# Block-sorted attention and routed two-layer network on one core: values sorted as rows through DRAM for pairs 4-15, half-chunk blocks, three query turns during the Sinkhorn

## The chip, the core and the metric

The kernel runs on one core of a Trainium2 chip. The metric is device microseconds of one execution: three runs of the kernel before took 748.79, 749.36 and 750.04 us, so the median is 749.36 us. A separate execution was recorded by the hardware profiler. Its span, from the first to the last instruction, is 748.4 us, and that same run was timed at 750.19 us, so 1.8 us lie outside the span.

## What is computed

Attention comes first. For each of 32 heads (4 batches x 8 heads), queries, keys and values have 768 rows of 64. A small 8x8 matrix is normalised five times by rows and columns ("Sinkhorn"), and the result mixes the eight 96-row blocks of keys and of values. Each block of queries then attends to its own mixed block. The output, with the heads side by side, is a 3072x512 matrix x that goes through eight experts, weighted by a second normalised matrix.

```python
for _ in range(5):                      # P = sort_net, per head 8 x 8
    P = np.exp(P - P.max(-1))           # first round subtracts the maximum
    P = P / P.sum(-1); P = P / P.sum(-2)
k_sorted = einsum('bhij,bhjcd->bhicd', P, k_b)     # blocks of 96 rows
v_sorted = einsum('bhij,bhjcd->bhicd', P, v_b)
attn = softmax(scale * q_b @ k_sorted.T)           # per block
x = (attn @ v_sorted)  ->  3072 x 512
G = exp(x @ w_gate); 8 rounds of row and column normalisation
out = sum_e G[:, e] * (relu(x @ w1[e]) @ w2[e])    # 8 experts, 512 -> 1024 -> 512
```

## The kernel before

Two heads form a pair, and there are 16 pairs. The order of the instructions on every engine is written out by hand. Each engine runs its own instructions in that order, so an instruction that waits holds up everything behind it on its engine.

**Start.** DVE (VectorE) and ACT (ScalarE) alternate through the five Sinkhorn rounds (L123 to L136). Meanwhile PE (TensorE) runs 24 matmuls on zeros (L115, "spins") whose results nobody reads. The last product is written sixteen times wide (`Prep`, L135). Eight matmuls spread it over the partitions (L140), DVE copies it out (`Pbig`, L143), and `build_r` multiplies it with a mask into the mixing matrix `R` (L156).

**The pair loop** (L281) runs iterations m = 0 to 19 as a software pipeline. Iteration m holds `stage1(m)`, `stage2(m-1)`, `stage3(m-2)` and `stage4(m-3)`, with a `fill(1)` behind each stage.

- `stage1` (L162) sorts keys and values: 12 matmuls each with `R` as the moving operand (L171) leave them transposed (`KT`, `VT`, 64 columns per head). It also turns the queries by 12 transposes (L182), and builds `R` of the next pair.
- `stage2` (L189) makes the scores (16 matmuls, L197), the exponentials on ACT, and turns `VT` back into rows by 8 transposes (L204). DVE copies them to `VS`, which has a column of ones beside each head.
- `stage3` (L209) multiplies attention and values (16 matmuls, L216). DVE divides by the sum that the ones gave (L219, L220) into `OG`.
- `stage4` (L223) turns `OG` by 8 transposes (L227), and ACT writes it into `xtT`, the transposed x.
- `fill` (L268) puts in one block of the first expert layer (`h_block`: 4 matmuls of 512 columns and a relu on ACT or DVE) as soon as the batch that the block reads is done (`state["done"]`). Until the first batch is done, at m = 6, it puts in one spin instead.
- `gate` (L232) makes the gate's logits of one batch.

POOL (GpSimd) issues all loads of q, k, v and of the weights; they are cast from float32 to bfloat16 on the way. Four pairs are loaded ahead into five buffers (L79, L285). The first-layer weights of experts 0 and 1 are loaded at m = 0 and m = 5, the second-layer weights of these experts at m = 8 and m = 11. SP (SyncE) issues the load of `sort_net` and, at the end, the stores.

**After the loop** come eight normalisation rounds of the gate, with three blocks each (L313), and then the experts: `y_tile` (second layer, 8 matmuls of 512 columns, L339) alternates with the remaining `h_block`s; ten buffers `hT` limit how far the first layer runs ahead. The last tile's store ends the kernel.

Of the kernel before, what the change touches and what calls it, by code (L numbers as in the profile page):

```python
# [25 lines left out]
def kernel(  # L26
# [17 lines left out]
    HB = 10  # L44
    scale = 1.0 / (D ** 0.5)
# [6 lines left out]
    ps = ctx.enter_context(tc.tile_pool(name="ps", bufs=8, space=bass.MemoryType.PSUM))  # L52

    def bank(shape, dt=F32):
        return ps.tile(shape, dt, name="bank")
# [8 lines left out]

# [6 lines left out]
    mask = ones.tile([128, 16], F32)  # L71
    nc.vector.reduce_sum(out=mask, in_=ident.rearrange("p (j c) -> p c j", c=16), axis=AX.X)
# [6 lines left out]
    iop = actx.enter_context(tc.tile_pool(name="iop", bufs=5))  # L79
    atp_ = actx.enter_context(tc.tile_pool(name="atp", bufs=2))  # L80
    qkv = {}

    def load_pair(m):
        r = []
        for src, nm in ((kh, "kb"), (vh, "vb"), (qh, "qb")):
            t = iop.tile([128, 2, 6, 64], BF16, name=nm)
            nc.gpsimd.dma_start(out=t, in_=src[2 * m:2 * m + 2].rearrange("h p kk d -> p h kk d"))  # L87
            r.append(t)
        qkv[m] = r
# [11 lines left out]
    for m in range(4):  # L101
        load_pair(m)
# [3 lines left out]
    xtT = ones.tile([128, 4, B, 6, 128], BF16)  # L106
    xf = xtT.rearrange("d hp b kk p -> d hp (b kk p)")
# [4 lines left out]


    w_ = bank([128, 512])
    for _ in range(24):  # L115
        nc.tensor.matmul(w_, wide[:, 0:128], wide, start=True, stop=True)

    rs = ones.tile([32, 8], F32)
    Prep = ones.tile([32, 8, 8, 16], BF16)
    Pt = P.rearrange("p i j -> p j i")  # L120
    nc.vector.reduce_max(out=rs, in_=P, axis=AX.X)
    nc.vector.tensor_sub(P, P, mkap(rs, [rs.ap[0], rs.ap[1], [0, 8]]))
    for it in range(5):  # L123
        nc.scalar.activation(out=P, in_=P, func=AF.Exp)
        nc.vector.reduce_sum(out=rs, in_=P, axis=AX.X)
        nc.vector.reciprocal(out=rs, in_=rs)
        nc.vector.tensor_tensor(out=P, in0=P, in1=mkap(rs, [rs.ap[0], rs.ap[1], [0, 8]]),
                                op=ALU.mult)
        nc.vector.reduce_sum(out=rs, in_=Pt, axis=AX.X)
        nc.vector.reciprocal(out=rs, in_=rs)  # L130
        if it < 4:
            nc.vector.tensor_tensor(out=Pt, in0=Pt, in1=mkap(rs, [rs.ap[0], rs.ap[1], [0, 8]]),
                                    op=ALU.mult)
        else:
            nc.vector.tensor_tensor(out=Prep, in0=mkap(P, [P.ap[0], [8, 8], [1, 8], [0, 16]]),  # L135
                                    in1=mkap(rs, [rs.ap[0], [0, 8], [1, 8], [0, 16]]), op=ALU.mult)  # L136

    pbp = bank([128, 8, 32])
    for i in range(8):
        nc.tensor.matmul(pbp[:, i, :], Prep[:, i].rearrange("g j c -> g (j c)"),  # L140
                         ident[0:32, 0:32], start=True, stop=True)
    Pbig = ones.tile([128, 8, 32], F32)
    nc.vector.tensor_copy(Pbig, pbp)  # L143


    KT, VT, QT, ATT, VS, OG = {}, {}, {}, {}, {}, {}

    vs_ = [ones.tile([96, 8, 2, 65], BF16, name=f"vs{n}") for n in range(2)]
    for t in vs_:
        nc.vector.memset(t[:, :, :, 64:65], 1.0)  # L150

    Rt = {}

    def build_r(m):
        R = Rt[m] = atp_.tile([128, 2, 8, 16], BF16, name="R")
        nc.vector.tensor_tensor(  # L156
            out=R,
            in0=mkap(Pbig, [Pbig.ap[0], [1, 2], [32, 8], [0, 16]], off=2 * m),
            in1=mkap(mask, [mask.ap[0], [0, 2], [0, 8], [1, 16]]),
            op=ALU.mult)  # L160

    def stage1(m):  # L162
        kb, vb, qb = qkv[m]
        R = Rt[m]
        for src, dic, nm in ((kb, KT, "KT"), (vb, VT, "VT")):
            dic[m] = atp_.tile([128, 8, 6, 16], BF16, name=nm)
            for kh2 in range(2):
                b_ = bank([128, 3, 128])
                for k3 in range(3):
                    for h2 in range(2):  # L170
                        nc.tensor.matmul(b_[64 * h2:64 * h2 + 64, k3, :], src[:, h2, 3 * kh2 + k3, :],  # L171
                                         R[:, h2].rearrange("p i c -> p (i c)"), start=True, stop=True)
                dst = dic[m][:, :, 3 * kh2:3 * kh2 + 3, :].rearrange("d i kk c -> d kk i c")
                b_ = b_.rearrange("d kk (i c) -> d kk i c", c=16)
                if nm == "KT" or kh2 == 0:
                    nc.scalar.copy(dst, b_)  # L176
                else:
                    nc.vector.tensor_copy(dst, b_)  # L178
        b_ = bank([128, 6, 128], BF16)
        for kk in range(6):  # L180
            for h2 in range(2):
                nc.tensor.matmul(b_[64 * h2:64 * h2 + 64, kk, :], qb[:, h2, kk, :], ident,  # L182
                                 is_transpose=True, start=True, stop=True)
        QT[m] = atp_.tile([128, 6, 128], BF16, name="QT")
        nc.vector.tensor_copy(QT[m], b_)
        if m + 1 < NPAIR:
            build_r(m + 1)

    def stage2(m):  # L189
        ATT[m] = [atp_.tile([96, 2, 384], BF16, name=f"at{h2}") for h2 in range(2)]  # L190
        for half in range(2):
            bb = [bank([96, 4, 96]) for _ in range(2)]
            for i4 in range(4):
                i = half * 4 + i4
                for h2 in range(2):
                    hs = slice(64 * h2, 64 * h2 + 64)
                    nc.tensor.matmul(bb[h2][:, i4, :], KT[m][hs, i].rearrange("d kk c -> d (kk c)"),  # L197
                                     QT[m][hs, :, 16 * i:16 * i + 16], start=True, stop=True)
            for h2 in range(2):
                nc.scalar.activation(out=ATT[m][h2][:, half, :], in_=bb[h2].rearrange("k i q -> k (i q)"),  # L200
                                     func=AF.Exp, scale=scale)
        b_ = bank([96, 8, 128], BF16)
        for i in range(8):
            nc.tensor.matmul(b_[:, i, :], VT[m][:, i].rearrange("d kk c -> d (kk c)"), ident, is_transpose=True,  # L204
                             start=True, stop=True)
        VS[m] = vs_[m % 2]
        nc.vector.tensor_copy(VS[m][:, :, :, 0:64], b_.rearrange("c i (h d) -> c i h d", d=64))

    def stage3(m):  # L209
        OG[m] = atp_.tile([96, 8, 2, 64], BF16, name="OG")  # L210
        for half in range(2):
            for h2 in range(2):
                b_ = bank([96, 4, 65])
                for i4 in range(4):
                    i = half * 4 + i4
                    nc.tensor.matmul(b_[:, i4, :], ATT[m][h2][:, half, 96 * i4:96 * i4 + 96],  # L216
                                     VS[m][:, i, h2, :], start=True, stop=True)
                rc = atp_.tile([96, 4], F32, name="rc")
                nc.vector.reciprocal(out=rc, in_=b_[:, :, 64:65].rearrange("q i a -> q (i a)"))  # L219
                nc.vector.tensor_tensor(out=OG[m][:, 4 * half:4 * half + 4, h2, :], in0=b_[:, :, 0:64],  # L220
                                        in1=mkap(rc, [rc.ap[0], [1, 4], [0, 64]]), op=ALU.mult)

    def stage4(m):  # L223
        b, hpi = m // 4, m % 4
        b_ = bank([128, 8, 96], BF16)
# [3 lines left out]
        nc.scalar.copy(xtT[:, hpi, b].rearrange("d kk (i c) -> d i kk c", c=16),  # L229
                       b_.rearrange("d i (kk c) -> d i kk c", c=16))  # L230

    def gate(b):  # L232
        b_ = bank([128, 6, E])
        for t in range(6):
            for kk in range(4):
                nc.tensor.matmul(b_[:, t, :], xtT[:, kk, b, t, :], wg[:, kk], start=(kk == 0),  # L236
# [7 lines left out]
    def h_block(e, c, fb, both=False):  # L244
        if fb == 0:
            hT[e, c] = hp_.tile([128, 8, 512], BF16, name="hTs")
        b_ = bank([128, 512])
        for kk in range(4):
            nc.tensor.matmul(b_, w1t[e][:, kk, fb * 128:(fb + 1) * 128], xf[:, kk, c * 512:(c + 1) * 512],  # L249
                             start=(kk == 0), stop=(kk == 3))  # L250
        flip[0] ^= 1
        if both and flip[0]:
            nc.vector.tensor_scalar_max(hT[e, c][:, fb, :], b_, 0.0)  # L253
        else:
            nc.scalar.activation(out=hT[e, c][:, fb, :], in_=b_, func=AF.Relu)  # L255

    early = [(0, 0), (1, 0), (0, 1), (0, 2), (1, 1), (1, 2), (0, 3), (1, 3), (0, 4), (0, 5), (1, 4), (1, 5)]
    seq = early + [(e, c) for e in range(2, E) for c in range(6)]
    blocks = [(e, c, fb) for e, c in seq for fb in range(8)]
    last_batch = [0, 1, 1, 2, 3, 3]  # L260
    state = {"h": 0, "done": -1}

    def spin(n):
        b_ = bank([128, 512])
        for _ in range(n):
# [140 lines left out]
```

The softmax here doesn't subtract the row's maximum and nothing guards it: scores larger than these inputs give would overflow.

## Time and profile before

| | |
|---|---|
| median of three runs | 749.36 us |
| span of the profiled execution | 748.4 us (that run: 750.19 us) |
| PE matmul records | 4588, busy 738.3 us |
| 1536 + 1536 matmuls of the two expert layers | 346.1 + 338.0 us busy |
| first sorting matmul of the pair loop | starts at 14.45 us |
| start of iterations m = 0 to 7 | 14.45, 18.33, 22.46, 26.33, 30.62, 35.06, 39.27, 43.49 us |
| length of an iteration with four blocks and no gate | 6.81 us |
| first matmul of the second layer | 146.8 us |
| end of the last DVE instruction | 745.05 us |

Start times in a row of the timeline are microseconds from the span's start. A "busy" PE is not a PE at its peak: durations of matmuls overlap, so what one costs in a stream is read from the distance between the starts of consecutive groups. 32 matmuls of 512 columns take 6.91 us in the second half of the kernel, so one costs 0.216 us there.

### The profile page before, as it was taken

Reading aid. Unit: us, or ns where it says so; the run is one execution under the profiler, and the core shown is the slowest. Engines: PE = TensorE matmul, PEld = TensorE weight load, DVE = VectorE, ACT = ScalarE, POOL = GpSimd, SP = SyncE. Lnnn points to the kernel's source line nnn. Section 1 sums busy time; section 2 is a strip of 40 time slices with the busy share of each in tenths; the row PEclk is TensorE's granted clock in tenths of the full one; section 3 lists DMA queues with packets and bytes.
Section 4 is the critical chain, followed back from the end, with each engine's and each line's share of the span. In section 5 each row is a group of like instructions: output and inputs, shape, how many; then the busy total and the mean of one; then the engine's idle time right before and its main releaser. Section 6 shows DMA issues by size and latency. Waiting matters only on the chain.

```text
span 748.4 us, 10663 instructions
## 1 busy us (share of the span) xinstructions
PE 738.3 (99%) x4588; PEld 358.5 (48%) x4588; DVE 252.1 (34%) x497; ACT 274.2 (37%) x497; POOL 48.9 (7%) x71
## 2 busy tenths in 40 slices
PE   6999999999999999999999999999999999999997
PEld 3776665444444444444444444444444444444443
DVE  5887775632122122122221221221221221212443
ACT  2776665513423423324324324234234233243000
POOL 8542000000000000000000000000000000000000
PEclk8999999999999999999999999999999999999999
DMA  9999100011300061200330032100330003000133
GB/s 149 204 205 163 19 2 1 1 20 38 56 1 1 0 96 29 46 1 1 56 57 1 0 57 40 19 0 1 57 56 1 1 0 57 1 0 1 43 154 141
DMA packets 29679, 33.21 MB, mean 44 GB/s; under 512 B 1984, under 2 KB 22464, under 8 KB 29632
## 3 DMA queue, kind: packets, MB, share of 16 engines
q0 software_dynamic: 26128, 26.23, 22.5%
q1 hardware_dynamic: 3504, 6.30, 2.2%
q8 instruction: 36, 0.59, 0.3%
q14 instruction: 11, 0.09, 0.0%
HBM read 52.45 MB, written 6.29 MB: 78 GB/s over the span
## 4 chain that ended last, share of the span: by engine, by line
PE 98%; DMA 1%; POOL 1%; DVE 0%; issue 0%; POOLq 0%
PE bank L249 44%; PE bank L339 44%; PE bank L171 2%; PE bank L216 2%; PE bank L204 1%; PE bank L197 1%; PE bank L266 1%; DMA qb<-in_q_dram 1%; PE bank L182 1%; PE bank L227 1%; PE bank L236 0%; POOL kb L87 0%; POOL vb L87 0%; PE bank L321 0%; POOL qb L87 0%; DVE osbl L345 0%
## 5 line engine op out<-in xcount | busy, mean ns | idle before, releaser
L255 ACT ACTIVATE hTs<-bank 128x512 bf16<-128x512 f32 x358 | 213.7, 597 | 371.2 <-PE bank L249 370.4
L249 PE MATMUL bank<-xtT,w1e 128*128 128x512 bf16 x1536 | 346.1, 379 | 0.0
L339 PE MATMUL bank<-w2e,hTs 128*128 128x512 bf16 x1536 | 338.0, 379 | 0.0
L345 DVE SCALAR_TENSOR_TENSOR osbl<-bank,glog,osbl 128x512 f32<-128x512 f32 x168 | 126.2, 751 | 398.7 <-PE bank L339 398.7
L339 PEld LDWEIGHTS <-hTs 128*128 128x128 bf16 x1536 | 150.2, 98 | 181.0
L249 PEld LDWEIGHTS <-w1e 128*128 128x128 bf16 x1536 | 147.9, 98 | 170.3
L342 DVE TENSOR_SCALAR osbl<-bank,glog 128x512 f32<-128x512 f32 x24 | 18.0, 751 | 54.7 <-PE bank L339 54.7
L220 DVE TENSOR_TENSOR OG<-bank,rc 96x256 bf16<-96x256 f32 x64 | 26.9, 421 | 2.2
L95 POOL DMA_DIRECT2D w1e<-in_moe_w_dram x8 | 6.0, 752 | 312.6 <-PE bank L249 312.3
L99 POOL DMA_DIRECT2D w2e<-in_moe_w_dram x8 | 7.1, 888 | 237.5 <-PE bank L339 237.1
L253 DVE TENSOR_SCALAR hTs<-bank 128x512 bf16<-128x512 f32 x26 | 17.7, 683 | 6.1 <-PE bank L249 6.1
L229 ACT COPY xtT<-bank 128x768 bf16<-128x768 bf16 x16 | 12.8, 798 | 14.1 <-PE bank L227 13.7
L176 ACT CAST KT<-bank 128x384 bf16<-128x384 f32 x32 | 13.8, 486 | 8.1 <-PE bank L171 7.9
L87 POOL DMA_DIRECT2D kb<-in_k_dram x16 | 11.5, 722 | 20.9 <-PE bank L171 20.1
L178 DVE CAST VT<-bank 128x384 bf16<-128x384 f32 x16 | 8.9, 553 | 11.2 <-PE bank L171 8.8
L219 DVE RECIPROCAL rc<-bank 96x4 f32<-96x4 f32 x64 | 10.9, 171 | 3.7 <-PE bank L216 3.7
L87 POOL DMA_DIRECT2D vb<-in_v_dram x16 | 11.5, 722 | 5.2 <-PE bank L266 2.5
L87 POOL DMA_DIRECT2D qb<-in_q_dram x16 | 11.6, 724 | 1.9 <-issue 0.3
L266 PE MATMUL bank<-wide 128*128 128x512 bf16 x28 | 10.6, 419 | 0.0
L204 PE MATMUL bank<-ident,VT 128*96 128x128 bf16 x128 | 10.4, 224 | 0.0
L171 PE MATMUL bank<-R,kb 128*64 128x128 bf16 x192 | 9.1, 234 | 1.0 <-DMA qb<-in_q_dram 1.0
L197 PEld LDWEIGHTS <-KT 64*96 64x96 bf16 x256 | 7.1, 121 | 5.8 <-issue 5.6
(152 smaller groups left out, 232.6 us busy)
## 6 DMA issues: line engine op xcount, KB each, us to landing
w1e<-in_moe_w_dram POOLq DMA_DIRECT2D x8, 1024.0 KB, 8.1
w2e<-in_moe_w_dram POOLq DMA_DIRECT2D x8, 1024.0 KB, 8.9
out_dram<-osbl SPq DMA_DIRECT2D x24, 256.0 KB, 2.0
kb<-in_k_dram POOLq DMA_DIRECT2D x16, 192.0 KB, 7.3
vb<-in_v_dram POOLq DMA_DIRECT2D x16, 192.0 KB, 7.3
qb<-in_q_dram POOLq DMA_DIRECT2D x16, 192.0 KB, 7.3
P<-in_sort_net_dram SPq DMA_DIRECT2D x1, 8.0 KB, 1.7
wg<-in_moe_w_gate_dram POOLq DMA_DIRECT2D x1, 8.0 KB, 6.8
```

The source lines that it names most:

```text
L87: nc.gpsimd.dma_start(out=t, in_=src[2 * m:2 * m + 2].rearrange("h p kk d -> p h kk d"))
L171: nc.tensor.matmul(b_[64 * h2:64 * h2 + 64, k3, :], src[:, h2, 3 * kh2 + k3, :], R[:, h2].rearrange("p i c -> p (i c)"), start=True, stop= ...
L204: nc.tensor.matmul(b_[:, i, :], VT[m][:, i].rearrange("d kk c -> d (kk c)"), ident, is_transpose=True, start=True, stop=True)
L216: nc.tensor.matmul(b_[:, i4, :], ATT[m][h2][:, half, 96 * i4:96 * i4 + 96], VS[m][:, i, h2, :], start=True, stop=True)
L220: nc.vector.tensor_tensor(out=OG[m][:, 4 * half:4 * half + 4, h2, :], in0=b_[:, :, 0:64], in1=mkap(rc, [rc.ap[0], [1, 4], [0, 64]]), op=AL ...
L249: nc.tensor.matmul(b_, w1t[e][:, kk, fb * 128:(fb + 1) * 128], xf[:, kk, c * 512:(c + 1) * 512], start=(kk == 0), stop=(kk == 3))
L253: nc.vector.tensor_scalar_max(hT[e, c][:, fb, :], b_, 0.0)
L255: nc.scalar.activation(out=hT[e, c][:, fb, :], in_=b_, func=AF.Relu)
L266: nc.tensor.matmul(b_, wide[:, 0:128], wide, start=True, stop=True)
L339: nc.tensor.matmul(b_, hT[e, c][:, fb, tt * 128:(tt + 1) * 128], w2t[e][:, fb, :], start=(fb == 0), stop=(fb == 7))
L342: nc.vector.tensor_scalar(out=osbl[:, t, :], in0=b_, scalar1=glog[:, t, e:e + 1], scalar2=None, op0=ALU.mult)
L345: nc.vector.scalar_tensor_tensor(out=osbl[:, t, :], in0=b_, scalar=glog[:, t, e:e + 1], in1=osbl[:, t, :], op0=ALU.mult, op1=ALU.add)
```

## The change

- **Values of pairs 4 to 15** (`MB = 4`). A second mixing matrix `Rv`, with its columns in another order, is the stationary operand of two matmuls of 384 columns. The result has rows as partitions (`VR`), and is copied out half by ACT and half by DVE. It is written to a DRAM tile `vd` by SP and read back, in the order that `stage3` wants, into `VS` (`v_back`, also SP). The 8 transposes of `VT` and the copy to `VS` fall away for these pairs.
- **Start.** The 24 spins become 4, and 6 in each Sinkhorn round. The queries of pairs 0 to 2 (`QA = 3`) are turned in rounds 1 to 3, copied out by ACT between two exponentials. The loads start with these queries. The wide product `Prep` is replaced by a narrow one (`Pb`), one matmul that turns it, and eight matmuls with a selection matrix `sel` (a copy on ACT). `R` of pair 0 is built from PSUM before `Pbig` is copied.
- **Blocks.** Chunk 1 of experts 0 and 1 and chunk 4 of expert 0 are cut into halves of 256 columns.
- **Buffers and order.** One PSUM tile of eight banks is handed out in turn. `stage3` takes two banks at a time and divides per head, not per head and half. Five pairs are loaded ahead into six buffers. The weight loads move: first layer to m = 1 and m = 4, second layer to m = 13 and m = 15, later first-layer weights to where the last block of the expert two before was issued. The gate of a batch comes at the end of m = 8, 12, 16, 19. The last tile of the second layer is cut into halves. Code for a DRAM path of the output (`XB = 16`) is not reached.

```diff
+    PS = ps.tile([128, 8, 512], F32)
+    def bank(dt=F32):
+        b_ = PS[:, turn[0] % 8, :]
+        turn[0] += 1
...
-    for m in range(4):
-        load_pair(m)
+    for src, m in ((qh, 0), (qh, 1), (kh, 0), (vh, 0), (qh, 2), (kh, 1), (vh, 1), (kh, 2), (vh, 2),
+                   (qh, 3), (kh, 3), (vh, 3)) + tuple((s_, m) for m in range(4, AH) for s_ in (kh, vh, qh)):
+        load(src, m)
...
-    for _ in range(24):
-        nc.tensor.matmul(w_, wide[:, 0:128], wide, start=True, stop=True)
+    sel = ones.tile([64, 64, 16], BF16)
+    nc.scalar.copy(sel, mkap(ident, [[ident.ap[0][0], 64], [1, 64], [0, 16]]))
+    spin(4)
     for it in range(5):
         nc.scalar.activation(out=P, in_=P, func=AF.Exp)
+        if 1 <= it <= QA:
+            q_turn(it - 1, "act")
+        spin(SQ_)
         nc.vector.reduce_sum(out=rs, in_=P, axis=AX.X)
...
-            nc.vector.tensor_tensor(out=Prep, in0=mkap(P, [P.ap[0], [8, 8], [1, 8], [0, 16]]),
-                                    in1=mkap(rs, [rs.ap[0], [0, 8], [1, 8], [0, 16]]), op=ALU.mult)
+        dst = Pt if it < 4 else Pb.rearrange("p (i j) -> p j i", j=8)
+        nc.vector.tensor_tensor(out=dst, in0=Pt, in1=rbi, op=ALU.mult)
+    nc.tensor.matmul(b_, Pb, ident[0:32, 0:32], start=True, stop=True)
+    nc.vector.tensor_copy(PT, b_)
+    for i in range(8):
+        nc.tensor.matmul(pbp[:, i, :], sel[:, 8 * i:8 * i + 8, :].rearrange("k j c -> k (j c)"), PT,
+                         start=True, stop=True)
+    build_r(0, pbp[:, :, 0:2].rearrange("p i g -> p g i"))
+    nc.vector.tensor_copy(Pbig, pbp.rearrange("p i g -> p g i"))
...
     def stage1(m):
+        sort_t(KT, "KT", kh, m, "aa")
+        if m < MB:
+            sort_t(VT, "VT", vh, m, "ad")
+        else:
+            VR = atp_.tile([128, 6, 2, 64], BF16, name="VR")
+            t = qkv[id(vh), m]
+            for h2 in range(2):
+                b_ = bank()[:, 0:384]
+                nc.tensor.matmul(b_, Rv[m][:, h2].rearrange("p c i -> p (c i)"),
+                                 t[:, h2].rearrange("p kk d -> p (kk d)"), start=True, stop=True)
+                b_ = b_.rearrange("p (kk d) -> p kk d", d=64)
+                if h2 == 0:
+                    nc.scalar.copy(VR[:, :, h2, :], b_)
+                else:
+                    nc.vector.tensor_copy(VR[:, :, h2, :], b_)
+            vd[m] = drp.tile([6, 128, 128], BF16, name="vd")
+            nc.sync.dma_start(out=vd[m].rearrange("kk p e -> p kk e"), in_=VR.rearrange("p kk h d -> p kk (h d)"))
+        if m >= QA:
+            q_turn(m, "dve")
...
+    def v_back(m):
+        if m >= MB:
+            VS[m] = vs_[m % 3]
+            nc.sync.dma_start(out=VS[m][:, :, 1:129],
+                              in_=vd[m].rearrange("kk (c i) e -> (kk c) i e", i=8))
...
+    early = [(0, 0, 0, 512), (1, 0, 0, 512), (0, 1, 0, 256), (1, 1, 0, 256), (0, 1, 256, 512), (1, 1, 256, 512),
+             (0, 2, 0, 512), (1, 2, 0, 512), (0, 3, 0, 512), (1, 3, 0, 512), (0, 4, 0, 256), (0, 4, 256, 512),
+             (0, 5, 0, 512), (1, 4, 0, 512), (1, 5, 0, 512)]
...
     for m in range(NPAIR + 4):
         if m < NPAIR:
             stage1(m)
-        if m + 4 < NPAIR:
-            load_pair(m + 4)
-        if m == 0:
+        if m + AH < NPAIR:
+            load(kh, m + AH)
+            load(vh, m + AH)
+            load(qh, m + AH)
+        if m == 1:
             load_w1(0)
-        if m == 5:
+        if m == W1B:
             load_w1(1)
-        if m == 8:
+        if m == 13:
             load_w2(0)
-        if m == 11:
+        if m == 15:
             load_w2(1)
-        fill(1)
+        fill(f[0], spins=SP_)
         if 1 <= m <= NPAIR:
             stage2(m - 1)
+        if m < NPAIR:
+            v_back(m)
...
+        if m in (6, 10, 14, 19 if XB < NPAIR else 18):
+            state["done"] += 1
+        fill(f[3], spins=SP_)
+        if m in (8, 12, 16, 19):
+            gate({8: 0, 12: 1, 16: 2, 19: 3}[m])
```

## The prediction

> **What bounds the kernel.** I read the page's slices first, then the chain of waits, then PE's timeline of one iteration.
>
> ```profile
> PE   6999999999999999999999999999999999999997
> PEclk8999999999999999999999999999999999999999
> DMA  9999100011300061200330032100330003000133
> PE 98%; DMA 1%; POOL 1%; DVE 0%; issue 0%; POOLq 0%
> ```
>
> From 14.45 us to the end PE is the chain: 98% of the span. So the end moves by what PE's work between is worth, and by when it starts. Two other things show: in the first slice the clock is not full, and in the first four slices the DMA engines are full. PE's own timeline prices the work. Iteration m = 8, with four blocks (columns: start, length, what):
>
> ```profile
> 50.89 0.53 PE L171 MATMUL bank<-R,kb 128*64 128x128 bf16 x12
> 51.25 0.50 PE L171 MATMUL bank<-R,vb 128*64 128x128 bf16 x12
> 51.59 0.50 PE L182 MATMUL bank<-ident,qb 128*64 128x128 bf16 x12
> 52.02 1.04 PE L249 MATMUL bank<-xtT,w1e 128*128 128x512 bf16 x4
> 52.99 0.56 PE L197 MATMUL bank<-QT,KT 64*96 64x96 bf16 x16
> 53.48 0.65 PE L204 MATMUL bank<-ident,VT 128*96 128x128 bf16 x8
> 53.96 1.03 PE L249 MATMUL bank<-xtT,w1e 128*128 128x512 bf16 x4
> 54.82 0.33 PE L216 MATMUL bank<-vs_194,at_1144 96*96 96x65 bf16 x4
> ```
>
> Distances between starts: key sort 0.36, value sort 0.34, query turn 0.43, scores 0.49, value transposes 0.48, a block 0.86. A block takes 0.97 where a stage with another array shape follows: a switch of shape costs about 0.1. An iteration takes 6.81, without its blocks 3.35; four spins (0.216 each) instead make 4.21, as iterations 5 and 6 show. No fill with a finished batch ever runs dry: all 28 spins of L266 lie in m = 0 to 6.
>
> The start is worse than its work. Stretches of the start (columns after the span: busy time of PE, PEld, DVE, ACT, POOL; then granted clock, DMA share, GB/s):
>
> ```profile
> 6.80:13.70 6.90, 2.90 (x20) 1.34 (x19) 5.26 (x20) 0.54 (x3) 5.68 (x8) 1.00 1.24 179
> 13.70:20.50 6.80, 6.05 (x77) 4.31 (x76) 2.69 (x8) 2.49 (x6) 4.60 (x7) 0.50 1.39 200
> ```
>
> PE has nothing to do from 9.34 to 13.11 us. Then the granted clock is 0.50 for 6.8 us, just when the pairs begin: a spin takes 0.43 instead of 0.216, and iterations 0 and 1 take 3.88 and 4.13.
>
> **The sum, against the span of 748.4.**
>
> (a) First sorting matmul. Before, the last exponential starts at 10.33 and `R` is ready at 14.39. ACT's new copy `sel` (64x1024) costs about 1.0 by the rows of 384 and 768 elements (0.487, 0.798) and waits for the identity at 2.47, so the first exponential moves from 2.95 to 3.5. A round is 1.81, so the next two are due at 5.3 and 7.1. Each query turn puts a copy of 0.80 (L229's row) on ACT ahead of the next exponential, and it needs its load. The first five loads landed at 4.9, 7.6, 8.5, 9.5 and 10.55 (issue plus time to landing). The queries of pairs 0, 1 and 2 become loads 1, 2 and 5. Turn 1 (7.6 + 0.8 for PE at a slow clock + 0.8) puts the fourth exponential at 9.2, and turn 2 (10.55 + 0.45 + 0.8) the fifth at 11.8. Then 1.51 to the last product as before, 0.26 for it (L132's row; `Prep` cost 1.21), 0.3 for one matmul and its hand-over, 0.2 for a small copy, 0.45 for eight matmuls, 0.45 for `R`: 15.1. That is +0.65. Bounds: 13.6 if no load is waited for and `sel` hides, 17 if every turn runs at the slow clock.
>
> (b) Iterations 0 to 6 took 29.04. At the full clock, with the queries of three pairs gone: m = 0: 0.36 + 0.34 + 0.86 + a switch or so = 1.70; m = 1 adds stage 2: 2.75; m = 2 is 4.21 without query turn and stage 4: 3.44; m = 3 is 4.21. At m = 4 values are sorted as rows: 384 columns are 0.162 by the 512-column price, twice 0.324, plus two switches of 0.10 (keys and queries beside it use the 64-column shape) against 0.34: +0.18, so 4.39. m = 5 also loses the transposes (0.48): 3.91. m = 6 the same, and one spin becomes a block (+0.65): 4.56. Together 24.96: -4.1. The bounds of the switch are 0 and 0.2 per pair, since the trace has no such sequence; I take 0.2, what the two observed switches cost. ACT needs 3.65 per iteration here (4.21 minus 0.56 idle, iteration 6) and DVE 4.2, less 0.6 when the copy to `VS` goes, plus 0.4 for `Rv`; neither exceeds PE by more than 0.3, which the eight banks absorb.
>
> (c) The rows of pairs 7 to 15: 9 x 0.18 = +1.6. The transposes of pairs 6 to 15: 10 x 0.48 = -4.8.
>
> (d) The block moved into m = 6 is missing later: -0.86.
>
> (e) Half blocks: 96 more matmuls. Their columns are the same; 128 columns cost 0.060 at L204 against 0.054 by the 512-column price, so 6 ns each at most: +0.3 (0 to 0.6). As no fill ran dry, they bring nothing.
>
> (f) Last tile in halves: DVE's last 0.75 becomes about 0.42 (L220's row of 256 elements), and a smaller store: -0.4 (0 to -0.6).
>
> Sum: 0.65 - 4.1 + 1.6 - 4.8 - 0.86 + 0.3 - 0.4 = -7.6. From the median 749.36 (0.83 below the profiled run's 750.19, of which 1.8 lie outside the span) this gives **741.8**.
>
> Costed at nothing: the fewer, wider divisions of `stage3` and the moved gate (DVE and ACT wait for PE in the blocks: 398.7 us at L345, 370.4 at L255), three memsets on POOL (0.2 each, ahead of loads needed 10 us later), second-layer weights at m = 13 and 15 (needed at 140, landing after 12 at most).
>
> **What the trip through DRAM hides behind.** Per pair SP issues a write and a read (0.38 each by the issue of `sort_net`), and its queue is empty until the first store at 705 us. The read waits for the write; behind it on SP is only the next pair's write. `VS` of pair 4 is wanted 2.6 us into m = 6, some 9.7 after `VR` is copied. A landing on an idle queue took 1.7 to 2.0; with the engines shared, say 3.4, twice, plus two issues: 7.6. So it hides with 2 us to spare, later with 6 or more. The other bound is the 7.3 median of the loads, which counts a queue eight deep: then pair 4 is 5.7 late.
>
> It also takes DMA engines that are full. Each trip is 2 x 768 runs of 256 bytes. Two neighbouring microseconds of the DMA view price them:
>
> ```profile
> DMA packets 278, 0.20 MB, mean 201 GB/s; under 512 B 17, under 2 KB 278, under 8 KB 278
> DMA packets 649, 0.19 MB, mean 185 GB/s; under 512 B 416, under 2 KB 649, under 8 KB 649
> w1e<-in_moe_w_dram POOLq DMA_DIRECT2D x1, 1024.0 KB, 12.2
> ```
>
> In the first, 261 load packets (1536 bytes read each) fill 16 engines: 61 ns apiece. In the second, 28 fewer of them made room for 399 packets of 16 bytes: 4 ns apiece. A 256-byte packet lies between 4 and 61; by bytes, 61 x 256/1536 + 4 = 14.5 ns, my value, so 0.7 us a leg. The third row is expert 1's weights: issued at 34.06, landed at 46.3, behind saturated loads. In the changed kernel the same loads stand before it, plus eight legs of pairs 4 to 7: 46.3 + 5.6 = 51.9. PE wants it in the ninth block, the last fill of m = 8: 40.1 + 6.5 + 5.6 = 52.2. It just arrives; every ns per packet above 15.3 costs 0.38 us.
>
> [...]
>
> **Rivals.**
>
> *The start is lost again.* PE still idles while the last round ends (about 1.3 us from 12.3), and waits for turn 2. Busy time before the boundary at 13.7 is some 4.6 of 6.8 us: between the 2.90 that led to half clock and the 6.05 that led to full. If it counts as idle, 15.1 to 20.5 runs at half clock: 5.4/2 = +2.7. With the first sort 1.5 later as well: 746. Still faster.
>
> [...] The one fall in this trace followed a gap of 3.77.
>
> *The trip starves the loads.* If 256-byte packets cost nearly what 1536-byte packets do, the first-layer weights and then the pairs come late, and PE stalls in order. Gain and loss cancel at 15.3 + 7.6/0.38 = 35 ns. At 61 ns the weights land at 46.3 + 23.4 = 69.7, 17.5 late: 759; at 45 ns: 753. For it: DMA share above 1.2 until 60 us. Against it: the 4 ns, and that loads past m = 8 have 9 us of slack. This is the slower case.
>
> *Rows don't pay.* If the switches and an exposed weight load eat the whole 0.48 per pair, 3.6 less is gained: 745.4. That is inside the range.
>
> **How the numbers follow.** The forecast with its own bounds (738.5 to 745) gets 0.62, the lost start (745 to 747.5) 0.18, the starving loads (above 749.4 mostly, 753 to 759) 0.14, and 0.06 is left for partial stalls that end near the old time. A measurement can tell 0.2%, or 1.5 us, from no change. So faster 0.80, same 0.06, slower 0.14. The range leaves the starving case out above and reaches 738 below (no switch cost -2.4, first sort at 14): 738 to 748.
>
> **What would show it.** Right: the clock stays at 1.00 from 7 us on; first sorting matmul near 15.1, m = 7 near 40; iterations of 6.5; ACT's fifth exponential just after the third turn's copy. Wrong: PE waiting for `w1e`, `vs` or `kb` between 28 and 90 us; a row of 0.50 after 13 us; switches of more than 0.1 round the two new matmuls; DMA packets under 512 bytes whose mean time is nearer 61 than 15 ns.

## The result and the profile after

The changed kernel takes 766.88 us (median of 4 runs, 766.69 to 767.78) against 749.24 us for the kernel before on the same chip: 1.0237 times as long, interval 1.0219 to 1.0254. The forecast was 741.8, the range ended at 748. The span of the profiled execution is 765.0 us, 16.6 more than before.

The slices of PE and of the granted clock (40 equal parts of the span, each digit in tenths), and the shares of the chain, on the page of the changed kernel:

```profile
PE   7959799999999999999999999999999999999998
PEclk9979899999999999999999999999999999999999
PE 92%; DMA 5%; issue 1%; DVE 1%; POOL 1%; ACT 0%; POOLq 0%; DVEq 0%; SPq 0%; ACTq 0%
```

PE fell from 98% of the chain to 92%, and DMA has 5%. PE's slices 3 and 5 are low, and the clock is with them. The waits name what PE stood for (columns: total, times, longest):

```profile
PE PS L274 <- DMA vs_264<-vd: 8.3, 1, 8.3
PE PS L274 <- DMA vs_263<-vd: 5.2, 1, 5.2
```

L274 is `stage3`, and `vs<-vd` is the sorted values coming back from DRAM. The timeline of PE shows both stands, of pair 4 in iteration 6 and of pair 9 in iteration 11 (in brackets the idle time and what ended it):

```profile
42.15 0.38 PE L134 MATMUL PS<-wide 128*128 128x512 bf16 x1
50.82 0.85 PE L274 MATMUL PS<-vs_264,at_766 96*96 96x65 bf16 x8 [8.29 <-DMA vs_264<-vd]
...
92.37 0.85 PE L274 MATMUL PS<-vs_263,at_1374 96*96 96x65 bf16 x8 [5.16 <-DMA vs_263<-vd]
```

After each stand PE runs at half clock. The stretches of the two stands and of what follows (busy time of PE, PEld, DVE, ACT, POOL, then granted clock, DMA share, GB/s):

```profile
42.50:50.80 8.30, 0.02 (x1) 0.00 (x0) 0.80 (x3) 1.23 (x4) 2.25 (x4) 0.71 1.21 198
50.80:56.20 5.40, 5.38 (x43) 3.28 (x43) 2.38 (x5) 1.36 (x3) 0.03 (x1) 0.50 1.29 195
...
87.20:92.40 5.20, 0.04 (x2) 0.03 (x1) 0.04 (x1) 0.84 (x3) 0.00 (x0) 0.80 0.96 148
92.40:97.10 4.70, 4.70 (x38) 3.90 (x39) 2.02 (x5) 1.18 (x2) 0.00 (x0) 0.50 0.46 85
```

5.4 and 4.7 us at half clock lose 2.7 and 2.4 us. A shorter wait of 0.9 us follows at 59.3 us, for pair 5. The profile puts it down to DVE, but the read of these values, issued at 54.88, landed 5.3 us later, at 60.2, just when the matmul starts. Together the trip's waits and the half clock behind them cost some 19 us on this trace.

The difference between the two traces, piece by piece (first matmuls of the iterations, and the end of the last DVE instruction: 745.05 before, 761.95 after):

| stretch | before | after | difference | forecast |
|---|---|---|---|---|
| to the first sorting matmul | 14.45 | 17.37 | +2.9 | +0.65 |
| iterations 0 to 5 | 24.82 | 22.60 | -2.2 | -4.4 |
| iteration 6 | 4.22 | 15.04 | +10.8 | +0.34 |
| iterations 7 to 14 | 55.63 | 62.92 | +7.3 | -2.4 |
| from iteration 15 on | 645.93 | 644.02 | -1.9 | -1.8 |

The SP queue shows the legs of the trip. A write is issued, the read waits for its landing, and the next pair's write stands behind the read:

```profile
32.81 0.40 SPq L243 DMA_DIRECT2D vd<-VR  x1
41.59 0.66 SPq L289 DMA_DIRECT2D vs_264<-vd  x1
42.34 0.57 SPq L243 DMA_DIRECT2D vd<-VR  x1
54.88 0.56 SPq L289 DMA_DIRECT2D vs_265<-vd  x1
...
73.35 0.59 SPq L243 DMA_DIRECT2D vd<-VR  x1
84.77 0.55 SPq L289 DMA_DIRECT2D vs_263<-vd  x1
```

The write of pair 4 is issued at 32.81; its read can go only at 41.59, and lands at 50.8: 8.7 and 9.2 us for the two legs that the forecast took for 3.4 each. Pair 5's rows lay ready at about 37.7, but their write had to wait behind that read until 42.34. For pair 9 the write alone took 11.4 us. Beside it, from POOL's timeline:

```profile
73.21 1.80 POOL L115 DMA_DIRECT2D w2e<-in_moe_w_dram  x2
```

Both second-layer loads go out at 73.2 us, in iteration 9, though they stand at m = 13 and 15 in the program: POOL goes through its own list as fast as its own waits let it, and behind the last pair's loads nothing held it.

### The profile page after: what moved, and what is told of

The parts are those of the page before. It is cut to its first block, busy times and chain, and to the rows that moved or that the text cites. A ratio compares the mean times of both kernels' runs of the same rounds, so it can differ in the third digit from the quotient of the medians.

```text
span 765.0 us, 10470 instructions
## 1 busy us (share of the span) xinstructions
PE 737.4 (96%) x4412; PEld 362.7 (47%) x4486; DVE 242.9 (32%) x440; ACT 277.9 (36%) x515; POOL 49.1 (6%) x74
## 4 chain that ended last, share of the span: by engine, by line
PE 92%; DMA 5%; issue 1%; DVE 1%; POOL 1%; ACT 0%; POOLq 0%; DVEq 0%; SPq 0%; ACTq 0%
PE PS L327 43%; PE PS L430 43%; PE PS L274 1%; DMA vs_264<-vd 1%; DMA vd<-VR 1%; DMA vs_263<-vd 1%; DMA vb<-in_v_dram 1%; DMA qb<-in_q_dram 1%; PE PS L216 1%; PE PS L257 1%; PE PS L305 1%; PE PS L143 1%; PE PS L235 1%; PE PS L314 0%; DVE OG L278 0%
## 5 line engine op out<-in xcount | busy, mean ns | idle before, releaser
L333 ACT ACTIVATE hTs<-PS 128x512 bf16<-128x512 f32 (+1 forms) x372 | 215.2, 579 | 397.7 <-PE PS L327 382.5
L327 PE MATMUL PS<-xtT,w1e 128*128 128x512 bf16 (+1 forms) x1595 | 346.5, 369 | 2.0 <-issue 0.2
L430 PE MATMUL PS<-w2e,hTs 128*128 128x512 bf16 (+1 forms) x1513 | 336.0, 378 | 1.6
L436 DVE SCALAR_TENSOR_TENSOR osbl<-PS,glog,osbl 128x512 f32<-128x512 f32 (+1 forms) x169 | 126.4, 748 | 398.3 <-PE PS L430 375.6
L433 DVE TENSOR_SCALAR osbl<-PS,glog 128x512 f32<-128x512 f32 x24 | 18.0, 751 | 51.2 <-PE PS L430 50.2
L331 DVE TENSOR_SCALAR hTs<-PS 128x512 bf16<-128x512 f32 (+1 forms) x36 | 20.3, 570 | 23.2 <-PE PS L327 22.1
L278 DVE TENSOR_TENSOR OG<-PS,rc 96x512 bf16<-96x512 f32 x32 | 22.0, 687 | 1.1
L134 PE MATMUL PS<-wide 128*128 128x512 bf16 x55 | 19.0, 462 | 1.4 <-DVE wide L85 1.2
L221 ACT CAST KT<-PS 128x384 bf16<-128x384 f32 x32 | 13.8, 484 | 9.7 <-PE PS L216 9.0
L307 ACT COPY xtT<-PS 128x768 bf16<-128x768 bf16 x16 | 12.7, 796 | 11.5 <-PE PS L305 10.7
L104 POOL DMA_DIRECT2D kb<-in_k_dram x16 | 11.5, 722 | 21.1 <-PE PS L235 10.6
L104 POOL DMA_DIRECT2D vb<-in_v_dram x16 | 11.7, 728 | 10.6 <-DMA w1e<-in_moe_w_dram 4.5
```

Source lines behind the costliest of these rows:

```text
L134: nc.tensor.matmul(b_, wide[:, 0:128], wide, start=True, stop=True)
L278: nc.vector.tensor_tensor(out=OG[m][:, :, h2, :].rearrange("q (f i) d -> q f i d", f=2), in0=b_[:, :, :, 1 - h2:65 - h2], in1=mkap(rc, [rc ...
L331: nc.vector.tensor_scalar_max(hT[e, c][:, fb, lo:hi], b_, 0.0)
L333: nc.scalar.activation(out=hT[e, c][:, fb, lo:hi], in_=b_, func=AF.Relu)
L430: nc.tensor.matmul(b_, hT[e, c][:, fb, tt * 128:(tt + 1) * 128], w2t[e][:, fb, ns], start=(fb == 0), stop=(fb == 7))
L433: nc.vector.tensor_scalar(out=osbl[:, t, ns], in0=b_, scalar1=glog[:, t, e:e + 1], scalar2=None, op0=ALU.mult)
```

## The experiments

All times stand beside runs of the kernel before on the same chip; the ratio to it is given with its 95% interval.

### Without the trip, and with its traffic alone

```diff
-    MB = 4
+    MB = 16
```

> All 16 pairs take the old way for the values (sorted with R, turned back by 8 transposes); everything else of the change stays. Theory 'the trip': PE stood still for the values coming back from DRAM (8.3, 5.2 and 0.9 us) and ran at half clock after the two long stands (2.7 and 2.4 us), 19.4 us together; without the trip these go and 12 x 0.30 us of PE work comes back: 766.9 - 19.4 + 3.6 = 751. Rival 'the pair loop': the new start, the ring of eight banks and the half blocks cost the time themselves: above 758.

Measured: 749.42 us, 1.0007 (0.9998 to 1.0017), 1.6 us below the theory's 751. Without the trip the whole loss, 17.5 us, is gone, and the rest of the change together gains nothing. The clock of this run never falls in the profiled execution (mean granted clock 1.00), and its first sorting matmul comes at 15.82. In the changed kernel's it came at 17.37, before any value goes to DRAM; so of the 17.5 us some 16 are the trip's, which is also what the 19 us above leave after the 12 x 0.30 us that the rows save.

```diff
+            vd[m] = drp.tile([6, 128, 128], BF16, name="vd")
+            nc.sync.dma_start(out=vd[m].rearrange("kk p e -> p kk e"), in_=QT[m])
...
+            nc.sync.dma_start(out=vj_[m % 3][:, :, 1:129], in_=vd[m]...)   # vj_ is read by nobody
```

> As the run without the trip, but SP still writes 192 KB per pair 4 to 15 to DRAM (the turned queries in place of the sorted values) and reads them back into a tile that nobody uses. Same packets, same queue, same moments, no reader. Theory 'the trip' (what costs is that PE waits for a long latency): same time as the run without the trip, 751, within 1.5. Rival 'the packets' (18,432 packets of 256 bytes take the DMA engines from the loads, which then come late): some 5 us or more above it, with PE waiting for kb, qb or w1e.

Measured: 759.31 us, 1.0139 (1.0124 to 1.0154), which would be the rival's number. But the trace names another wait:

```profile
DVE QT L149 <- DMA vd<-QT: 10.7, 2, 9.7
```

DVE waited up to 9.7 us for a `QT` buffer's write to DRAM to land before it filled that buffer again; the experiment had built a new wait of its own. It was repeated with six buffers for `QT`.

> Repeats the run with traffic and no reader, whose own trace showed a new wait: the turned queries had four buffers, and each had to be written to DRAM before it could be used again. Now they have six. Theory 'the trip' (the cost is PE's wait for a latency, not the packets): as without the trip, 749.4, within 1.5. Rival 'the packets' (the loads come late because of 18,432 small packets): 754 or more, with PE waiting for kb, qb or w1e.

Measured: 749.38 us, 1.0006 (0.9996 to 1.0016), within 0.1 us of the run without the trip. So 18,432 packets of 256 bytes on the same queue cost no time that shows. The moments are the same only at first: the legs of pair 4 and the write of pair 5 are issued at 31.39, 40.03 and 40.75 us, 1.4 to 1.6 us ahead of those of the changed kernel, but pair 6's read at 67.80 instead of 60.40, and later ones fall further back, where fewer loads run. Those first three legs take 8.6, 10.6 and 13.6 us with no reader, as long as in the changed kernel (8.7, 9.2 and 12.5), and after 28 us PE waits for no load, here or in the changed kernel. What costs is that somebody waits for the trip: the rival that I had named for the slower side is out, and the latency is in.

### The second stand, and the third query turn

```diff
         if m == 13:
+            nc.gpsimd.tensor_copy(gt, KT[12][:, 0, 0, 0:1])
             load_w2(0)
```

> The changed kernel with one edit: POOL first reads one column of the sorted keys of pair 12 before it issues the first second-layer load, so that these two loads start in iteration 13 and not right behind the last pair's loads at 73 us. Theory: the second stand (5.2 us at 87 us, plus 2.4 us at half clock) comes from pair 9's trip sharing the DMA engines with these 4 MB of reads; it goes: 759.3. Rival: the stand comes from SP's queue, in which each write stands behind the read of the pair before, and stays: 766 to 767.

Measured: 761.22 us, 1.0159 (1.0142 to 1.0176). The stand at 87 us is gone; left are 9.1 us for pair 4 and 1.9 us for the pair behind it. So the second stand was the weights' doing. The 2 us above the expectation are that longer rest, and a second stretch at half clock after it (the granted clock is 0.63 from 62 to 66 us; the eight transposes at 62.31 us take 0.84 us, those at 70.11 take 0.51).

```diff
-    QA = 3
+    QA = 2
```

> The changed kernel with two query turns beside the Sinkhorn and the third back in the pair loop. Theory: the third turn waited for the fifth load (11.1 us), PE went to half clock, twelve spins at half clock kept the first matmul of the new mixing chain back from 14.3 to 15.95; without it the first sorting matmul comes at about 14 instead of 17.4, 0.43 us of PE work comes back: 764. The stand for pair 4 stays about 8 us long, since its write also starts earlier. Rival: the clock drop doesn't come from this wait, first sort stays above 16.5: 766 to 767.

Measured: 765.52 us (763.08 to 767.18), 1.0215 (1.0192 to 1.0239): between the two expectations, and not settled by the time. The first sorting matmul does come at 14.14, as expected without the third turn, but the clock falls at some 14.3 us in this execution (the key sort that starts at 14.14 takes 0.70 us where the full clock gives 0.53), so a fall there doesn't need that turn's wait, and iterations 0 and 1 take 3.1 us each; and the stands (9.6, 1.4 and 4.7 us) swallow what is left.

### More time for the trip

The values are sorted two iterations earlier, and each write goes ahead of the read before it:

```diff
-        else:
+        if MB <= m + VA < NPAIR:        # VA = 2
+            m += VA
             VR = atp_.tile([128, 6, 2, 64], BF16, name="VR")
...
-            v_back(m)
+            v_back(m + 1)
```

> The values still go through DRAM for pairs 4 to 15, but they are sorted two iterations earlier (their loads are there by then), SP issues the write of pair m+2 ahead of the read of pair m+1, VS has five buffers and the trip's DRAM tile four, and the second-layer loads start in iteration 13. Theory 'the trip': two legs of 9 us now have four iterations (17 us or more) instead of two (9.7), so no stand for vs is left, the clock stays up, and 12 x 0.30 us of PE work is won against the run without the trip: 745.8, at most 749 if pair 4 is still some us late. Rival: the trip costs by its packets or by SP's queue however early it starts: above 755.

Measured: 759.89 us, 1.0149 (1.0134 to 1.0164): a miss. The waits of this run show where the stand went:

```profile
ACT VR L246 <- DMA vd<-VR: 12.0, 3, 5.9
...
PE PS L135 <- ACT VR L246: 5.5, 1, 5.5
PE PS L274 <- ACT VR L246: 2.7, 1, 2.7
```

With two `VR` buffers, ACT's copy of a later pair waits for the write of an earlier one to land; PE needs ACT and stands too.

```diff
-            VR = atp_.tile([128, 6, 2, 64], BF16, name="VR")     # 2 buffers
+            VR = vrp.tile([128, 6, 2, 64], BF16, name="VR")      # 4 buffers
```

> The run with the values sorted two iterations earlier, but with four buffers for the sorted rows VR instead of two (and four for VS instead of five). In that run PE waited for ACT's copies into VR (2.7, 5.5, 0.7, 1.9 us): the wait had moved from the read's landing to the write's, since a VR buffer is free only when its write has landed. Theory: with four buffers this wait goes too: 746 to 749. Rival: two legs of 9 us one behind the other on SP hold less than one pair per iteration, so any number of buffers fills up: above 754.

Measured: 755.94 us, 1.0089 (1.0075 to 1.0103), above the theory and nearer to the rival. That wait is gone. PE now waits 1.5 us for the load of a pair's values, which are wanted earlier, and this is left of the trip (a wait of this run, then two of its writes in the view of DMA issues, whose last column is the time to landing):

```profile
PE PS L285 <- DMA vs<-vd: 6.9, 3, 5.2
```

```profile
vd<-VR SPq DMA_DIRECT2D x1, 192.0 KB, 11.9
...
vd<-VR SPq DMA_DIRECT2D x1, 192.0 KB, 15.9
```

The first write, issued at 22.6 us, takes 11.9 us, where the changed kernel's, issued at 32.8, took 8.7, and the one at 35.3 us takes 15.9: started earlier, the legs become longer. Two loads issued in the same microsecond as that first write took 12.7 and 14.1 us, the one beside the changed kernel's took 8.5. Buffers and lead move the stand about, but legs of 11.9 and 15.9 us stay too slow for an iteration of 4 to 6.5 us.

### The trip on idle engines

```diff
     def load(src, m):
+        if m >= AH:
+            qkv[id(src), m] = qkv[id(src), m % AH]
+            return
```

> The changed kernel without the loads of q, k and v for pairs 5 to 15 (these pairs use the tiles of pairs 0 to 4 again, so this part of the input is left out), and with the second-layer loads in iteration 13. The trip stays as the change has it: pairs 4 to 15, two iterations. Theory 'full engines': a leg takes 9 us only because the loads keep the 16 DMA engines full; with them idle from some 30 us on a leg takes about 3 us, PE never waits for vs, and the time is that without the trip less 12 x 0.30: 745.8, at most 747. Rival 'too short a way': two legs and SP's waits between them don't fit into two iterations of 4 us whatever else runs: PE waits for vs at pair 4, 5 or 6, 752 or more.

Measured: 746.84 us, 0.9963 (0.9950 to 0.9977). The trip stands as the change has it, two iterations, SP in the same order, and PE waits 0.3 us for it in all. The DMA issues of this run (last column: median us to landing):

```profile
vd<-VR SPq DMA_DIRECT2D x12, 192.0 KB, 2.6
vs<-vd SPq DMA_DIRECT2D x12, 192.0 KB, 3.8
```

2.6 and 3.8 us: the forecast's 3.4 fits engines that are idle, and the same trip stalls PE, for 8.3 us at pair 4, when the loads run beside it. The run takes away the loads' reads from DRAM along with their work on the engines, so it doesn't part these two.

```diff
-    MB = 4
+    MB = 11      # and the second-layer loads in iteration 13
```

> The change as it was, with its short way of two iterations, but only for pairs 11 to 15, and the second-layer loads in iteration 13. Their trips run when the pairs' loads are through. Theory: on idle DMA engines a leg takes some 3 us, nothing waits, and 5 x 0.30 us are won against the run without the trip: 747.9. Rival: a trip stalls PE wherever it stands: 752 or more.

Measured: 748.55 us, 0.9988 (0.9979 to 0.9997). The legs take 3.6 and 4.0 us (medians of five), PE never waits for them, and 0.9 of the expected 1.5 us show. One write, beside the second-layer loads, still takes 9.3 us (issued at 87.49, its read at 96.83): iterations of 6.6 us and more have room for that.

### What else in the change took its gain back

The gains in this and the next section are differences of medians. Measured from the kernel before on each run's own chip they come out 0.1 to 0.4 us larger (0.31 us above it without the trip, 0.92 below with late trips, 1.20 and 1.12 below in the next two runs, 3.14 in the one behind them).

Eight tiles for the eight banks, and `stage3` as before the change:

```diff
-    PS = ps.tile([128, 8, 512], F32)
-        b_ = PS[:, turn[0] % 8, :]
+        return ps.tile([128, 512 if dt == F32 else 1024], dt, name="PS")   # 8 buffers
...
-        for h2 in range(2):
-            b_ = bank2()[0:96, :, 0:260]...
+        for half in range(2):
+            for h2 in range(2):
+                b_ = bank()[0:96, 0:260]...
```

> Without the trip, and with the eight banks as eight tiles again; stage 3 divides per half and head as before the change. Theory: the ring of banks in one tile with two-bank divisions makes ACT wait for DVE (0.8 us before each xtT copy), which is why iterations 3 to 6 took 4.5, 4.8, 4.6 and 5.6 us instead of 4.2, 4.2, 4.2 and 4.9; these 2.1 us come back: 747.3. Rival: they come from the load on DVE and ACT: 749.4 or more, since the divisions of before take DVE longer.

Measured: 748.05 us, 0.9988 (0.9979 to 0.9998): 1.4 us below the run without the trip, of 2.1 expected. From iteration 3 to 7 it takes 18.2 us instead of 19.6. ACT's copy into `xtT`, in the timeline of the run without the trip and then of this one:

```profile
38.28 0.80 ACT L307 COPY xtT<-PS 128x768 bf16<-128x768 bf16 x1 [0.81 <-DVE rc L277]
```

```profile
37.48 0.80 ACT L298 COPY xtT<-PS 128x768 bf16<-128x768 bf16 x1 [0.56 <-PE PS L296]
```

In the first, ACT waits for a reciprocal on DVE that it has no use for; in the second, for PE's transposes, which it reads. The edit changed the tiles and the size of the divisions together, so which of the two made the wait wasn't tried apart.

```diff
-    nc.scalar.copy(sel, mkap(ident, ...))          # ahead of the first exponential
...
-        if 1 <= it <= QA:
-            q_turn(it - 1, "act")
-        spin(SQ_)
+        if it == 0:
+            nc.scalar.copy(sel, mkap(ident, ...))
+        if 2 <= it <= 3:
+            q_turn(it - 2, "act")
+        spin((6, 6, 6, 6, 8)[it])
```

> Without the trip, and with a start that waits for no load: the copy sel comes after the first exponential, two query turns (not three) stand in rounds 2 and 3, when their loads have landed, and two more spins follow the last exponential. Theory: the start lost time to the wait for the fifth load and to sel (first sorting matmul at 15.8 and 17.4 instead of 15.1 and 14.4): it comes at 13.4, one query turn of 0.43 us returns to PE: 747.4. Rival: the clock falls in the shorter start as it did in the run with two turns, iterations 0 and 1 run at half clock: 749 to 750.

Measured: 748.13 us, 0.9985 (0.9976 to 0.9995), 1.3 us below the run without the trip, of 2.0 expected. The first sorting matmul comes at 14.30 instead of 15.82, the clock stays up (mean granted clock 1.00), and iterations 3 to 6 give 0.6 us of it back.

### The pieces put together

Banks, start and whole blocks together, without the trip:

```diff
-(0, 1, 0, 256), (1, 1, 0, 256), (0, 1, 256, 512), (1, 1, 256, 512),
+(0, 1, 0, 512), (1, 1, 0, 512),
...
-(0, 4, 0, 256), (0, 4, 256, 512),
+(0, 4, 0, 512),
```

> No trip; eight tiles for the banks and divisions per half; the start that waits for no load; whole blocks. The three gains seen or expected singly (1.4 for the banks, 1.3 for the start, 0.25 for whole blocks, all against 749.4): 746.5. Rival: the gains overlap, since an earlier start runs into the same limit of DVE and ACT in iterations 3 to 6: 747.5 to 748.

Measured: 746.33 us, 0.9961 (0.9948 to 0.9973), 3.1 us below the run without the trip: the gains add up. Whole blocks weren't tried alone.

The same with all trips of pairs 4 to 15, two iterations ahead and with four buffers:

> The same, with the values of pairs 4 to 15 through DRAM, sorted two iterations ahead with four buffers each. Theory: 12 x 0.30 less than the run without the trip: 743, if no wait is left. Rival: the trip's waits come back because the pairs follow each other faster: 750 or more.

Measured: 755.33 us, 1.0080 (1.0066 to 1.0094): the rival. PE now waits longer for a load, too:

```profile
PE PS L233 <- DMA vb<-in_v_dram: 3.0, 1, 3.0
PE PS L277 <- DMA vs<-vd: 2.4, 2, 1.7
```

Values that are sorted two iterations earlier are also needed two iterations earlier, and the loads don't come faster.

Last, the fastest version with pairs 11 to 15 through DRAM (`MB = 11`, second-layer loads in iteration 13):

> The fastest version so far (no trip, eight tiles for the banks, the start that waits for no load, whole blocks: 746.3), and pairs 11 to 15 through DRAM, with the second-layer loads in iteration 13. Late trips alone gave 0.9 of the 1.5 us expected. Theory: the same here, 745.0 to 745.5. Rival: with faster iterations the late trips meet loads that are still running: 746.3 or more.

Measured: 745.77 us, 0.9951 (0.9937 to 0.9965), the fastest of all, 3.7 us below the kernel before. Its legs take 3.6 and 3.9 us. Against the version without any trip (746.33, in another set of runs) it gains 0.6, and the two intervals overlap, so this last step isn't shown.

## Why the prediction was wrong

**The step that failed** is in "What the trip through DRAM hides behind": "with the engines shared, say 3.4, twice, plus two issues: 7.6. So it hides with 2 us to spare". The legs took 8.7 and 9.2 us, and pair 4 came 8.3 us late. The text had the other bound before it, the loads' 7.3 us, "then pair 4 is 5.7 late", and set it aside because it "counts a queue eight deep". SP's queue was empty, but the engines behind it were not (DMA share 1.28 while the write of pair 4 ran, 1.20 while its read did): the row to price the leg by was that of transfers on full engines, and the same text said that the engines are full. That bound got no place in the range and no case of its own but the 0.06 for "partial stalls that end near the old time". It was too short as well: 7.3 a leg, where 8.7 and 9.2 were measured. From 741.8 to 766.9 it is 25.1 us; on the profiled execution the three waits for the trip make 14.4 of them, the half clock behind two of them 5.1, the start 2.3, and iterations 0 to 5 another 2.2.

**The slower rival had the right place and the wrong mechanism.** It let the trip's packets delay the loads. The run with traffic and no reader shows 0.0 us for that, and in the changed kernel itself PE waits for no first-layer weights and for no load of a pair behind the start. The packets' price, 14.5 ns by estimate, wasn't the issue.

**Costed at nothing and not nothing:** the second-layer weights "at m = 13 and 15". They left at 73.2 us, since nothing on POOL waits for these iterations, and they made the second stand (5.2 us and 2.4 at half clock; without it 5.7 us less). The forecast looked only at when they are needed, and not at whom they meet.

**The half clock** was foreseen for the start alone. It came after both stands, and added 5 us to 14.

**Start: +0.65 forecast, +2.9 measured.** (The terms of the sum give 14.97, not 15.1.) The chain up to the last product went as written (fifth exponential at 12.37 instead of 11.8, because the fifth load landed at 11.06, not 10.55). But PE's spins are in front of the first matmul of the new chain. Part of PE's timeline at the start of the changed kernel:

```profile
11.11 0.53 PE L143 MATMUL PS<-ident,qb 128*64 128x128 bf16 x12 [1.99 <-DMA qb<-in_q_dram]
11.79 4.22 PE L134 MATMUL PS<-wide 128*128 128x512 bf16 x11 [0.16 <-issue]
15.95 0.20 PE L179 MATMUL PS<-ident,Pb 32*64 32x32 bf16 x1
```

The same three rows in the run with traffic alone (four `QT` buffers), whose start is the same:

```profile
11.02 0.53 PE L143 MATMUL PS<-ident,qb 128*64 128x128 bf16 x12 [2.01 <-DMA qb<-in_q_dram]
11.70 2.54 PE L134 MATMUL PS<-wide 128*128 128x512 bf16 x11 [0.16 <-issue]
14.27 0.20 PE L179 MATMUL PS<-ident,Pb 32*64 32x32 bf16 x1
```

`Pb` is ready at 14.3 us (13.88 plus 0.43), and its matmul waits until 15.95 for twelve spins (one record is missing), most of which take 0.4 us each at half clock (granted clock 0.54 from 11.8 to 15.5 us). The clock fell at 11.8 us, after PE's wait for the third turn's load, and was back at 1.00 from 15.5. That the clock falls here is not in every execution: with the same start, the runs without the trip, with its traffic alone and with separate banks keep it and sort first at 15.7 to 16.2 us. So some 1.3 us of the delay belong to the chain, the rest to the clock.

**Iterations 0 to 5: -4.4 forecast, -2.2 measured.** The claim that "neither exceeds PE by more than 0.3, which the eight banks absorb" failed: iterations 3 to 5 took 4.5, 5.3 and 4.1 us instead of 4.2, 4.4 and 3.9. (Iterations 0 to 2 took the other 0.8.) The wider divisions of `stage3` were "costed at nothing" by DVE's and ACT's waits for PE at L345 and L255; but these lines are the expert layers, and neither runs in iterations 0 to 5. The run with separate banks and divisions per half, which has no trip, got 1.4 us back.

**Right:** the price of the rows (6.81 + 0.18 - 0.48 = 6.51 by the forecast; iterations 9 and 10 take 6.55 and 6.56 us); that half blocks bring nothing (iteration 13, all of them halves, takes 6.65); the block moved into iteration 6 and the shorter end (-1.9 in all from iteration 15 on, forecast -1.8). With the trip on idle engines the kernel takes 746.8 us, 5 us above the forecast. The start has no part in them there (first sort at 14.77, forecast 15.1). In its profiled execution iterations 0 to 5 take 22.6 us as in the changed kernel, 2.2 too many, iteration 6 takes 0.6 too many and 7 to 14 another 1.1; the last 1.6 are the distances of the profiled executions from the medians, 0.83 before and 0.74 here.

## What to carry to other kernels

Price a transfer by one of the same stretch, not by the queue it is put on, and ask whether its reader has slack for that: on the same SP queue a leg took 2.6 and 3.8 us without the later loads, and 8.7 and 9.2 for pair 4 beside them. A path that costs nothing in the first case was a stand of 8.3 us in the second, and each of the two long stands here cost again at half clock, 2.7 and 2.4 us. A place late in the program is no moment: the loads that stand at m = 13 and 15 left POOL at 73.2 us, in iteration 9, because nothing in front of them waited for those iterations. An experiment that adds traffic can also add the wait for its source buffer, 9.7 us here; look for it in the trace before reading the time.

## What the runs showed of the hardware

One microsecond (47 to 48) of the changed kernel, DMA queues with packets, MB and share of the engines:

```profile
q0 software_dynamic: 192, 0.14, 89.9%
q1 hardware_dynamic: 188, 0.05, 35.6%
```

The loads' queue and the trip's queue move packet for packet, 192 against 188 here and 380 against 381 from 34 to 36 us of the run with four `VR` buffers, though a load's packet reads 1536 bytes (384 values of float32) and the other 256. At that pace the 768 packets of a leg need 4.1 us. What sets the pace isn't shown. Most of the rest of the 8.7 us is a wait ahead of the first packet: between the issue at 32.81 and 36 us none of the write's packets is in the trace, only loads'. What it waits for isn't shown.

Alone, in the run without the later loads, 774 such packets, of a read and the next write, moved in one microsecond (36 to 37): at most 20.7 ns each on 16 engines, where the forecast had worked out 14.5.

The granted clock fell at 11.8 us after a wait of 1.99 us in one execution, and not after a wait of 2.01 us at the same place in the run with traffic alone. In the run with two turns it fell at some 14.3 us, and PE's longest gap from 7.87 us to there was 0.79 us. The fall in the kernel before had followed a gap of 3.77 us; here two came without such a gap, so gaps shorter than 3.77 us don't rule a fall out. The forecast's boundary at 13.7 us, with the busy time of the 6.8 us ahead of it deciding, was an estimate from two stretches of the kernel before; what sets the moment of a fall isn't shown.
